# First batch's loads, first-stage PSUM banks, and the order and width of block sums in a linear-attention and mixture kernel

## Chip, cores, metric

One core of one Trainium2 chip. The metric is device time of one execution in microseconds; lower is better.

## The reference

A linear attention without softmax, with a normalisation by row, feeds four dense experts whose outputs are mixed by given probabilities. All data are fp32.

```python
kv  = einsum('bhsd,bhse->bhde', k, v)            # 8 batches, 8 heads, 576 rows, 64 columns
o   = einsum('bhsd,bhde->bhse', q, kv)
x   = o / sqrt(mean(o*o, -1) + 1e-6) * g_norm    # then heads side by side: x is 4608 x 512
p   = probs / probs.sum(-1)
out = sum over e of p[:, e] * (relu(x @ w1[e]) @ w2[e])   # w1: 512 x 1024, w2: 1024 x 512, 4 experts
```

## The kernel before

Each matrix product is done by two nested levels of a seven-product scheme (Strassen's form): blocks of w1, w2 and x are added and subtracted ahead ("block sums"), and products are added into the output blocks behind. x is handled in nine chunks of 512 rows. Expert 0 works through the nine chunks while the attention of the next batch runs in between; experts 1 to 3 read the chunks' x blocks back from DRAM. A pair of expert and chunk is a "step", 36 in all.

The kernel does not write instructions in order. It hands operations with a key (a place) and a cost to a planner, which simulates the engines and emits each engine's order. The parts that matter here:

```python
def either(n):        # a block sum may go to VectorE or to GpSimd, whichever is free in the plan
    return {"DVE": 0.17 + 0.00108 * n, "POOL": 0.1 + 0.0025 * n}
...
BANKS = {"ub": 4, "db": 2, "ab": 2}              # PSUM banks: up products, down products, attention
...
def weights_1(e, key, step):                     # w1 of expert e: four loads, then block sums
    ...
    form(key + 4 * step, 5, 21, 4, ALU.add)      # 1024-wide sums, both inputs in SBUF
    form(key + 5 * step, 6, 5, 1, ALU.subtract)
    form(key + 6 * step, 7, 1, 21, ALU.subtract)
    form(key + 7 * step, 3, 2, 6, ALU.subtract)
    for j, m in enumerate(OUTER):                # then four 256-wide sums for each of seven blocks
        k2 = key + (8 + j) * step
        ...combine(k2, either(HN), ...)
...
def total(a, t, src, add_, ...):                 # adds a product out of PSUM: VectorE only
    nc.vector.tensor_tensor(out=block(whole, a, t), in0=src.ap[:, 0:HN], in1=add_.ap[:], op=ALU.add)
...
attention(0, -2.0, 1.3, 0.1)
weights_1(0, -0.9, 0.02)
x_views = {0: x_forms(0, -0.2, 0.02)}
...
        if e + 1 < E and c == NCH - 1:           # next expert's weights, during the last chunk
            weights_1(e + 1, s + 0.0, 0.12)
            weights_2(e + 1, s + 1.0, 0.12)
```

Lines are named by number in the profiles (in some runs an edit shifts them by one or two). Before and after: block sums L276 and L279; up products L697 and L713; PSUM-fed sums L718 and L737; down products L831 and L850; merges into the output L784/L788 and L803/L807; attention's scaling L432 and L440, its powers L425 and L433.

## Time and profile before

| | before |
|---|---|
| median | 1820.93 us (6 runs, 1818.36 to 1821.4) |
| TensorE busy | 98% of 1818.3 us |
| work of TensorE at its steady pitch | 1757 us |
| lost by TensorE up to 130 us / 500 us / end | 44 / 52 / 57 us |
| each change of expert | 1.5 us lost |

"Lost" is a count of mine that the prediction sets up: the time on the clock, less the matmul records started by then, each at its steady pitch. Waits and a slow clock both show in it, which busy time does not do.

### The profile page before, as it was taken

How to read it: one execution, taken by the hardware profiler on the slowest of the kernel's cores; microseconds unless marked ns; L12 is line 12 of the kernel's file. 1: busy time of each engine (PE TensorE's matmuls, PEld its weight loads, DVE VectorE, ACT ScalarE, POOL GpSimd, SP SyncE). 2: the span in 40 equal slices, each digit the busy share in tenths (PEclk: the TensorE clock that was granted, in tenths of full speed). 3: DMA queues.
4: the chain of work that ended last, by engine and by line, in shares of the span. 5: the costliest groups of instructions: out<-in, count | busy, mean ns of one | idle time of the engine just before them, and what ended most of it. 6: DMA issues, size and time to landing. Idle time of an engine off the chain costs nothing.

```text
span 1818.3 us, 32290 instructions
## 1 busy us (share of the span) xinstructions
PE 1784.6 (98%) x12496; PEld 1660.7 (91%) x12496; DVE 1126.2 (62%) x1841; ACT 608.4 (33%) x1345; POOL 475.1 (26%) x426
## 2 busy tenths in 40 slices
PE   5899999999999999999999999999999999999999
PEld 4889999999999999999999999999999999999997
DVE  6866665666676555555666555555566655556554
ACT  2544344443333333333333333333333333333331
POOL 4565554646364000000145000000036100000001
PEclk7999999999999999999999999999999999999999
DMA  9764444424433333334434333333434333343321
GB/s 231 179 167 141 128 139 126 135 95 139 132 109 119 117 114 115 114 113 134 136 130 152 118 118 118 118 118 121 147 127 163 117 115 117 118 118 116 115 74 35
DMA packets 192089, 228.96 MB, mean 126 GB/s; under 512 B 54464, under 2 KB 123328, under 8 KB 191936
## 3 DMA queue, kind: packets, MB, share of 16 engines
q1 hardware_dynamic: 191936, 226.89, 40.9%
q8 instruction: 99, 1.62, 0.4%
q14 instruction: 54, 0.44, 0.1%
HBM read 160.18 MB, written 66.65 MB: 125 GB/s over the span
## 4 chain that ended last, share of the span: by engine, by line
PE 94%; DVE 2%; SPq 2%; DMA 1%; issue 1%; POOL 0%; ACT 0%; DVEq 0%; ACTq 0%
PE ub L697 42%; PE db L831 29%; PE ab L831 18%; SPq L282 1%; PE ab L504 1%; PE ab L486 1%; DVE big L276 1%; PE ab L514 1%; PE ab L471 1%; DVE small L276 0%; DMA big<-in_moe_w_dram 0%; DMA small<-in_q_dram 0%; PE ab L553 0%; DVE big L718 0%; POOL big L276 0%
## 5 line engine op out<-in xcount | busy, mean ns | idle before, releaser
L831 PE MATMUL db<-big,big 128*128 128x256 f32 x2520 | 596.3, 380 | 1.7 <-DVE big L276 1.3
L697 PEld LDWEIGHTS ub<-small,big 128*128 128x128 f32 x3816 | 498.4, 192 | 23.4 <-issue 1.4
L697 PE MATMUL ub<-small,big 128*128 128x128 f32 x3816 | 513.5, 276 | 0.4 <-DVE big L718 0.4
L276 DVE TENSOR_TENSOR big<-big,big 128x1024 f32<-128x1024 f32 x343 | 474.8, 1384 | 55.1 <-ACT big L680 33.2
L831 PEld LDWEIGHTS db<-big,big 128*128 128x128 f32 x2520 | 455.2, 190 | 51.7 <-DVE big L276 1.5
L276 POOL TENSOR_TENSOR big<-big,big 128x1024 f32<-128x1024 f32 x85 | 209.0, 2462 | 1116.7 <-DVE big L276 976.1
L710 ACT ACTIVATE snap<-ub 128x256 f32<-128x256 f32 x756 | 285.5, 383 | 556.7 <-PE ub L697 500.8
L718 DVE TENSOR_TENSOR big<-ub,snap 128x256 f32<-128x256 f32 x756 | 307.0, 421 | 216.7 <-PE ub L697 163.1
L697 PE MATMUL ub<-small,w1y 128*128 128x128 f32 x2916 | 384.9, 276 | 2.2 <-DVE big L718 2.1
L697 PEld LDWEIGHTS ub<-small,w1y 128*128 128x128 f32 x2916 | 360.5, 192 | 7.9 <-DVE big L718 2.9
L831 PE MATMUL ab<-big,big 128*128 128x256 f32 x1512 | 357.4, 380 | 1.7 <-DVE small L788 1.7
L831 PEld LDWEIGHTS ab<-big,big 128*128 128x128 f32 x1512 | 273.2, 190 | 32.0 <-DVE small L788 2.1
L710 ACT ACTIVATE big<-ub 128x256 f32<-128x256 f32 x252 | 96.7, 384 | 414.6 <-PE ub L697 410.1
L788 DVE SCALAR_TENSOR_TENSOR small<-db,p_all,small 128x256 f32<-128x256 f32 x243 | 116.9, 481 | 139.8 <-PE db L831 139.2
L788 DVE SCALAR_TENSOR_TENSOR small<-ab,p_all,small 128x256 f32<-128x256 f32 x189 | 91.1, 482 | 177.3 <-PE ab L831 177.3
L680 ACT ACTIVATE big<-big 128x1024 f32<-128x1024 f32 x144 | 152.0, 1055 | 107.8 <-DVE big L276 104.8
L784 DVE TENSOR_SCALAR small<-db,p_all 128x256 f32<-128x256 f32 x72 | 34.6, 481 | 54.1 <-PE db L831 54.1
L425 POOL TENSOR_TENSOR rt<-ss,mhalf 128x8 f32<-128x8 f32 (+1 forms) x40 | 65.7, 1643 | 3.3
L421 POOL TENSOR_SCALAR ss<-ss 128x8 f32<-128x8 f32 (+1 forms) x40 | 15.6, 391 | 101.0 <-DVE ss L416 99.6
L416 DVE TENSOR_REDUCE ss<-small 128x8 f32<-128x512 f32 (+1 forms) x40 | 27.1, 678 | 22.3 <-ACT small L411 22.3
L504 PE MATMUL ab<-kvbd,small 128*128 128x128 f32 x256 | 38.3, 298 | 1.6 <-ACT kvbd L494 1.6
L432 DVE TENSOR_TENSOR small<-ab,rt 128x512 f32<-128x512 f32 (+1 forms) x40 | 27.4, 686 | 17.3 <-POOL rt L425 17.1
(63 smaller groups left out, 664.0 us busy)
## 6 DMA issues: line engine op xcount, KB each, us to landing
small<-x SPq DMA_DIRECT2D x189, 256.0 KB, 3.5
small<-x SPq DMA_DIRECT2D x189, 192.0 KB, 2.9
o<-small SPq DMA_DIRECT2D x108, 256.0 KB, 2.0
small<-o SPq DMA_DIRECT2D x108, 256.0 KB, 2.8
big<-in_moe_w_dram SPq DMA_DIRECT2D x32, 512.0 KB, 5.0
x<-small SPq DMA_DIRECT2D x63, 256.0 KB, 3.1
small<-in_q_dram SPq DMA_DIRECT2D x72, 128.0 KB, 3.9
kv<-in_k_dram SPq DMA_DIRECT2D x32, 288.0 KB, 3.5
```

Source lines behind the costliest of these rows:

```text
L276: lambda eng: adder(eng).tensor_tensor(out=out_(), in0=a(), in1=b(), op=op),
L416: lambda eng: nc.vector.reduce_sum(out=ss.ap[0:n, :], in_=rows(sq), axis=AX.X),
L425: nc.gpsimd.tensor_tensor(out=rt.ap[0:n, :], in0=ss.ap[0:n, :], in1=mhalf[0:n, :], op=ALU.pow)
L432: lambda eng: nc.vector.tensor_tensor(out=rows(x), in0=rows(raw), in1=rt.ap[0:n, :].unsqueeze(2).to_broadcast([n, H, D]), op=ALU.mult,),
L504: nc.tensor.matmul(raw.ap[:, rs], lhsT=qT.ap[:, rs], rhs=kb.ap[:])
L680: lambda eng: nc.scalar.activation(out=b.ap[:], in_=b.ap[:], func=ACT.Relu),
L697: nc.tensor.matmul(ps.ap[:, u * P:(u + 1) * P], lhsT=w1f[e][m][mm][1]()[:, u * P:(u + 1) * P], rhs=views[m][mm][1](), start=(mm in (1, 2, ...
L710: lambda eng: nc.scalar.activation(out=where(), in_=ps.ap[:, 0:HN], func=ACT.Copy),
L718: lambda eng: nc.vector.tensor_tensor(out=block(whole, a, t), in0=src.ap[:, 0:HN], in1=add_.ap[:], op=ALU.add),
L784: nc.vector.tensor_scalar_mul(out=acc[i].ap[:, cols], in0=ps.ap[:, 0:HN], scalar1=prob)
L788: nc.vector.scalar_tensor_tensor(out=acc[i].ap[:, cols], in0=ps.ap[:, 0:HN], scalar=prob, in1=acc[i].ap[:, cols], op0=ALU.mult, op1=ALU.add,)
L831: nc.tensor.matmul(ps.ap[:, 0:HN], lhsT=four(h[m])[:, kt // 2, t, kt % 2, :], rhs=w2f[e][m].ap[:, kt * HN:(kt + 1) * HN], start=(m in (1, ...
```

## The change

Its intent: start TensorE earlier, by bringing the first batch's data ahead of the weights and using idle banks for its attention; then order the block sums by when their products need them, and merge some of them. The diff is cut to its main lines; lines that begin with `#` are comments of this text, and `...` marks what is left out within a line.

```diff
+    def add(..., after=()):                     # an op may be placed behind another in the plan
-  if len(free[k]) < n + (self.SPARE.get(k, 0) if op.key > front + 0.1 else 0):
+  if len(free[k]) < n + (self.SPARE.get(k, 0) if eng == "SP" and op.key > front + 0.1 else 0):
-    BANKS = {"ub": 4, "db": 2, "ab": 2}
+    BANKS = {"u1": 2, "u2": 2, "db": 2, "ab": 2}
 # weights_1: places by need, for every expert
-        form(key + 4 * step, 5, 21, 4, ALU.add)
-        form(key + 5 * step, 6, 5, 1, ALU.subtract)
-        form(key + 6 * step, 7, 1, 21, ALU.subtract)
-        form(key + 7 * step, 3, 2, 6, ALU.subtract)
+        form(need + 0.25, 5, 21, 4, ALU.add)
+        form(need + 0.26, 6, 5, 1, ALU.subtract)
+        form(need + 0.5, 7, 1, 21, ALU.subtract)
+        form(need + 0.5, 3, 2, 6, ALU.subtract)
-            k2 = key + (8 + j) * step
+            need + j / 7                         # (the 256-wide sums of block j)
 # first batch: its own buffers, loads first, other banks
-            kt, vt, qt = Buf("kv", f"k{n}"), Buf("kv", f"v{n}"), Buf("small", f"q{n}")
+            kind = "kv" if b or hp < 2 else "big"
+            kt, vt, qt = Buf(kind, f"k{n}"), Buf(kind, f"v{n}"), Buf("small", f"q{n}")
+            want = at(hp) - 0.25 if b else key - 1 + 0.1 * hp
+            ...Buf("ab" if b else "u1"...), Buf("ab" if b else "db"...), Buf("ab" if b else "u2"...)
 # x blocks: one 256-wide and two 128-wide sums for four 128-wide ones
-            for o, a, b in ((5, 12, 1), (6, 3, 5), (7, 3, 12), (4, 2, 6)):
+            combine(key + j / 7, either(2 * P), ...)
+            for o, a, b in ((6, 3, 5), (4, 2, 6)):
 # up products: at most about two blocks open
+                    after=last[-2:-1] if mm in (1, 2) else (),
 # calls
-    weights_1(0, -0.9, 0.02)
-    x_views = {0: x_forms(0, -0.2, 0.02)}
+    weights_1(0, -2.5, 0.02, -0.35)
+    x_views = {0: x_forms(0, -0.3)}
-                weights_1(e + 1, s + 0.0, 0.12)
+                weights_1(e + 1, s + 0.0, 0.12, s + 0.6)
```

More of the change, by code (lines that the diff above doesn't have):

```diff
@@ L49, in __init__, with add @@
         self.ops = []
-    def add(self, key, cost, fn, reads=(), writes=(), parts=(), kb=0):
+    def add(self, key, cost, fn, reads=(), writes=(), parts=(), kb=0, after=()):
         op = Op(key, cost, fn, reads, list(writes) + list(parts), kb)
+        for o in after:
+            op.deps[o] = True
         for b in reads:
@@ L67, in add @@
         self.ops.append(op)
+        return op
     def layout(self, slots):
@@ L278, in combine, with load @@
         )
-    def load(key, buf, dst, src, kb, reads=()):
+    def load(key, buf, dst, src, kb, reads=(), also=()):
         plan.add(
             key, SPC, lambda eng: nc.sync.dma_start(out=dst(), in_=src), reads=reads,
-            parts=[buf], kb=kb,
+            parts=[buf] + list(also), kb=kb,
         )
@@ L330, in w2_src, with weights_1 @@
         return rows.rearrange("(kt p) d -> p kt d", p=P)
-    def weights_1(e, key, step):
+    def weights_1(e, key, step, need):
         f = {n: Buf("big", f"w1_{e}_{n}") for n in (1, 2, 21, 4, 5, 6, 7, 3)}
+        corner = {}
         for i, (n, dh, uh) in enumerate(((1, 0, 0), (2, 1, 0), (21, 0, 1), (4, 1, 1))):
+            corner[n] = Buf(None, f"w1c_{e}_{n}")
             load(
@@ L338, in weights_1 @@
                 lambda n=n: f[n].ap[:].rearrange("p (k u) -> p k u", k=2),
-                w1_src(e, dh, uh), 512,
+                w1_src(e, dh, uh), 512, also=[corner[n]],
             )
         def form(k_, o, a, b, op):
+            corner[o] = Buf(None, f"w1c_{e}_{o}")
             combine(
                 k_, either(1024), lambda: f[o].ap[:], lambda: f[a].ap[:], lambda: f[b].ap[:], op,
-                [f[a], f[b]], [f[o]],
+                [f[a], f[b], corner[a], corner[b]], [f[o], corner[o]],
             )
-        form(key + 4 * step, 5, 21, 4, ALU.add)
-        form(key + 5 * step, 6, 5, 1, ALU.subtract)
-        form(key + 6 * step, 7, 1, 21, ALU.subtract)
-        form(key + 7 * step, 3, 2, 6, ALU.subtract)
+        form(need + 0.25, 5, 21, 4, ALU.add)
+        form(need + 0.26, 6, 5, 1, ALU.subtract)
+        form(need + 0.5, 7, 1, 21, ALU.subtract)
+        form(need + 0.5, 3, 2, 6, ALU.subtract)
         w1f[e] = {}
         for j, m in enumerate(OUTER):
-            x, y = f[m], Buf("w1y", f"w1y_{e}_{m}")
+            x, low, y = f[m], corner[m], Buf("w1y", f"w1y_{e}_{m}")
             parts = {}
-            for n, at, (uq, kt) in ((1, 0, (0, 0)), (2, 1, (0, 1)), (7, 2, (1, 0)), (4, 3, (1, 1))):
-                parts[n] = (x, lambda x=x, uq=uq, kt=kt: two(x.ap[:])[:, kt, uq * HN:(uq + 1) * HN])
+            for n, (uq, kt) in ((1, (0, 0)), (2, (0, 1)), (7, (1, 0)), (4, (1, 1))):
+                parts[n] = (
+                    [x, low] if n == 7 else [x],
+                    lambda x=x, uq=uq, kt=kt: two(x.ap[:])[:, kt, uq * HN:(uq + 1) * HN],
+                )
             for n, at in ((5, 0), (6, 1), (3, 2)):
-                parts[n] = (y, lambda y=y, at=at: y.ap[:, at * HN:(at + 1) * HN])
-            k2 = key + (8 + j) * step
+                parts[n] = ([y], lambda y=y, at=at: y.ap[:, at * HN:(at + 1) * HN])
             for o, a, b, op in (
@@ L365, in weights_1 @@
                 combine(
-                    k2, either(HN), parts[o][1], parts[a][1], parts[b][1], op,
-                    [parts[a][0], parts[b][0]], [parts[o][0]],
+                    need + j / 7, either(HN), parts[o][1], parts[a][1], parts[b][1], op,
+                    parts[a][0] + parts[b][0], [low] if o == 7 else [y],
                 )
@@ L445, in attention @@
             n = f"{b}_{hp}"
-            kt, vt, qt = Buf("kv", f"k{n}"), Buf("kv", f"v{n}"), Buf("small", f"q{n}")
+            kind = "kv" if b or hp < 2 else "big"
+            kt, vt, qt = Buf(kind, f"k{n}"), Buf(kind, f"v{n}"), Buf("small", f"q{n}")
+            want = at(hp) - 0.25 if b else key - 1 + 0.1 * hp
             def kv_rows(t):
-                return t.ap[0:KP, :].rearrange("p (h j d) -> p h j d", h=2, d=D)
+                return t.ap[0:KP, 0:2 * KR * D].rearrange("p (h j d) -> p h j d", h=2, d=D)
             for r in range(2):
                 load(
-                    at(hp) - 0.25, qt,
+                    want, qt,
                     lambda qt=qt, r=r: qt.ap[:].rearrange(
@@ L459, in attention @@
                 load(
-                    at(hp) - 0.25, t,
-                    lambda t=t: t.ap[0:KP, :].rearrange("p (h x) -> p h x", h=2),
+                    want, t,
+                    lambda t=t: t.ap[0:KP, 0:2 * KR * D].rearrange("p (h x) -> p h x", h=2),
                     src[b, hs].rearrange("h (p j) d -> p h (j d)", j=KR), 288,
@@ L479, in attention @@
             )
-            bank = Buf("ab", f"kv{n}")
+            bank = Buf("ab" if b else "u1", f"kv{n}")
             kvbd[hp] = Buf("kvbd", f"kvbd{n}")
@@ L497, in attention @@
             plan.add(at(hp), {"ACT": 0.5}, diagonal, reads=[bank], writes=[kvbd[hp]])
-            raw = Buf("ab", f"raw{n}")
+            raw = Buf("ab" if b else "db", f"raw{n}")
             def attend(eng, raw=raw, qT=qT, kb=kvbd[hp]):
@@ L508, in attention @@
             scaled(at(hp + 0.4), n, raw, P, x)
-            bank = Buf("ab", f"xT{n}")
+            bank = Buf("ab" if b else "u2", f"xT{n}")
             def turn_x(eng, bank=bank, x=x):
@@ L587, with x_forms @@
     kept = {}
-    def x_forms(c, key, step):
+    def x_forms(c, key):
         xh = x_halves(c)
@@ L601, in x_forms @@
             combine(
-                key + j * step, either(NT), blocks[o][1], blocks[a][1], blocks[b][1], ALU.subtract,
+                key + (0.25, 0.26, 0.65, 0.8)[j], either(NT), blocks[o][1], blocks[a][1], blocks[b][1], ALU.subtract,
                 [blocks[a][0], blocks[b][0]], [blocks[o][0]],
@@ L611, in x_forms @@
                 parts[n] = (src, lambda ap=ap, kt=kt, th=th: ap()[:, kt, th * P:(th + 1) * P])
-            for n, at in ((5, 0), (6, 1), (7, 2), (4, 3)):
+            for n, at in ((5, 0), (7, 1), (6, 2), (4, 3)):
                 parts[n] = (t, lambda t=t, at=at: t.ap[:, at * P:(at + 1) * P])
-            for o, a, b in ((5, 12, 1), (6, 3, 5), (7, 3, 12), (4, 2, 6)):
+            combine(
+                key + j / 7, either(2 * P), lambda t=t: two(t.ap[:, 0:2 * P]),
+                lambda ap=ap: ap()[:, :, P:2 * P], lambda ap=ap: two(ap()[:, 0, :]),
+                ALU.subtract, [src], [t],
+            )
+            for o, a, b in ((6, 3, 5), (4, 2, 6)):
                 combine(
-                    key + (4 + j) * step, either(P), parts[o][1], parts[a][1], parts[b][1],
-                    ALU.subtract, [parts[a][0], parts[b][0]], [parts[o][0]],
+                    key + j / 7, either(P), parts[o][1], parts[a][1], parts[b][1],
+                    ALU.subtract, [parts[a][0], parts[b][0]], [t],
                 )
@@ L626, in x_forms @@
             plan.add(
-                key + 0.5, {"SP": 0.16}, store_raw, reads=[src], parts=[kept[c, m]], kb=192,
+                key + 0.9, {"SP": 0.16}, store_raw, reads=[src], parts=[kept[c, m]], kb=192,
             )
             plan.add(
-                key + 0.5, SPC,
+                key + 0.9, SPC,
                 lambda eng, t=t, keep=keep: nc.sync.dma_start(out=keep[:, 3 * P:], in_=t.ap[:]),
@@ L651, in x_again @@
                 for n, b, at in (
-                    (1, r, 0), (2, r, 1), (3, r, 2), (5, t, 0), (6, t, 1), (7, t, 2), (4, t, 3)
+                    (1, r, 0), (2, r, 1), (3, r, 2), (5, t, 0), (7, t, 1), (6, t, 2), (4, t, 3)
                 )
@@ L658 @@
     hidden = {}
+    last = []
     def four(b):
@@ L686, in up @@
             whole = made[m] = Buf("big", f"m{n}")
-            bank = {1: Buf("ub", f"u1_{n}"), 2: Buf("ub", f"u2_{n}")}
+            bank = {1: Buf("u1", f"u1_{n}"), 2: Buf("u2", f"u2_{n}")}
             snap = {}
@@ L691, in up @@
                 if mm == 5:
-                    bank[2] = Buf("ub", f"u3_{n}")
+                    bank[2] = Buf("u2", f"u3_{n}")
                 ps = bank[1 if mm in (1, 6, 7, 4) else 2]
@@ L701, in product @@
                         )
-                plan.add(
-                    key, pe(2, P), product, reads=[w1f[e][m][mm][0], views[m][mm][0]], writes=[ps]
-                )
+                op = plan.add(
+                    key, pe(2, P), product, reads=w1f[e][m][mm][0] + [views[m][mm][0]], writes=[ps],
+                    after=last[-2:-1] if mm in (1, 2) else (),
+                )
+                if mm == 3:
+                    last.append(op)
                 def copy(to, where, ps=ps, key=key):
@@ L853 @@
     attention(0, -2.0, 1.3, 0.1)
-    weights_1(0, -0.9, 0.02)
-    x_views = {0: x_forms(0, -0.2, 0.02)}
+    weights_1(0, -2.5, 0.02, -0.35)
+    x_views = {0: x_forms(0, -0.3)}
     weights_2(0, 0.0, 0.02)
-    norm_probs(0.1)
+    norm_probs(0.3)
     for e in range(E):
@@ L867 @@
                 if e == 0 and c + 1 < NCH:
-                    x_views[s + 1] = x_forms(c + 1, s + 0.75, 0.03)
+                    x_views[s + 1] = x_forms(c + 1, s + 0.7)
                 else:
```

## The prediction

> **What bounds the kernel now.** I read the page first, then a table of busy times by stretch of the span, then the waits of the first 60 us, then the timeline of VectorE and GpSimd where VectorE is slow. The page has TensorE busy 98% and its clock low only at the beginning, so I cut the span into stretches:
>
> ```profile
> core 0: us, PE busy (x) PEld busy (x) DVE busy (x) ACT busy (x) POOL busy (x), PEclk, DMA share, GB/s
> 0.00:18.00 18.00, 9.96 (x76) 8.50 (x76) 2.99 (x12) 4.55 (x9) 2.55 (x8) 1.00 0.90 225
> 18.00:42.00 24.00, 12.43 (x91) 10.30 (x91) 21.04 (x35) 6.01 (x13) 16.43 (x15) 0.58 0.99 235
> 42.00:60.00 18.00, 14.88 (x123) 13.67 (x123) 17.26 (x29) 7.16 (x18) 14.50 (x18) 0.88 0.97 255
> 60.00:86.00 26.00, 23.84 (x244) 22.64 (x242) 20.60 (x32) 14.61 (x35) 9.12 (x7) 0.95 0.49 119
> 86.00:105.00 19.00, 18.43 (x158) 16.43 (x160) 13.75 (x26) 8.88 (x20) 18.08 (x19) 1.00 0.56 139
> 105.00:500.00 395.00, 394.51 (x3117) 363.94 (x3112) 254.43 (x428) 159.49 (x357) 207.29 (x236) 1.00 0.45 135
> 500.00:1814.00 1314.00, 1310.61 (x8703) 1225.21 (x8702) 795.90 (x1285) 407.73 (x895) 207.13 (x126) 1.00 0.37 118
> 1814.00:1818.30 4.30, 0.00 (x0) 0.00 (x0) 0.28 (x1) 0.00 (x0) 0.00 (x0) 0.85 0.47 107
> ```
>
> From 105 us on TensorE is full. Busy time hides slow clocks, so I count its work at the steady pitch of the chain of waits: 16 up-projection records took 1.79 us (0.112 each), 8 down-projection records 1.73 (0.216), one batch's attention about 12.3 us in all. The program has 7056 and 4032 such records and 8 batches: 788 + 871 + 98 = 1757 us. TensorE ends at 1813.8, so 56.6 us are lost and 4.5 us are tail. Counting the records finished by a given time, the loss is 13 us at 18, 31 at 41.8 (where the first up product starts), 37 at 60, 42 at 86, 43 at 105, 44 at 130, 52 at 500, 57 at the end. **Three quarters of what can be won lies before 86 us**; the rest is spread thin over 1700 us.
>
> What TensorE waits for in the first 60 us:
>
> ```profile
> PE ab L514 <- DVE small L432: 8.8, 3, 4.3
> PE ab L471 <- DMA small<-in_q_dram: 5.8, 1, 5.8
> PE ub L697 <- DVE big L718: 3.1, 2, 2.7
> PE ab L486 <- DMA kv<-in_v_dram: 1.8, 2, 1.6
> ```
>
> It waits for VectorE: the scaling of attention (L432), then block sums (L718). In 18 to 60 us VectorE is busy 38.3 of 42 us. But part of that is waiting, as the timeline of VectorE shows, beside GpSimd's in the same microseconds:
>
> ```profile
> 75.27 0.68 DVE L276 TENSOR_TENSOR small<-big 128x512 f32<-128x512 f32 x1
> 75.87 2.45 DVE L276 TENSOR_TENSOR small<-big,small 128x128 f32<-128x128 f32 x1
> 78.25 0.28 DVE L276 TENSOR_TENSOR small<-small 128x128 f32<-128x128 f32 x1
> ...
> 79.52 2.44 DVE L276 TENSOR_TENSOR small<-big,small 128x128 f32<-128x128 f32 x1
> ```
>
> ```profile
> 75.50 2.67 POOL L276 TENSOR_TENSOR big<-big,big 128x1024 f32<-128x1024 f32 x1 [4.38 <-DVE big L718]
> 79.45 2.35 POOL L276 TENSOR_TENSOR big<-big,big 128x1024 f32<-128x1024 f32 x1 [1.28 <-ACT big L680]
> ```
>
> A 128-wide sum of 0.28 us takes 2.4 us, until GpSimd's 1024-wide sum is done. So block sums with both inputs in SBUF run on one of the two engines at a time.
>
> **What the Trainium skill says.** "SBUF — State Buffer", section "Who interferes with whom": a VectorE instruction with two SBUF inputs contends with a GpSimd instruction that reads SBUF, and the later one blocks for the whole instruction. The lines above agree; so does the PSUM-fed sum (L718), which one SBUF input leaves out of it: 756 of them, none slower than 0.43 us. "GPSIMD Engine Reference", section "3.1 Elementwise — side-by-side cycle accounting", puts a two-input sum on GpSimd at 1.96 times VectorE's time; here the 1024-wide means are 2462 and 1384 ns, 1.8 times with VectorE's blocked ones in. "TensorE: Matmul & The Clock Gate", section "Part 1: The HAM clock gate", has TensorE at half clock until it has been busy some 3.4 us, and again after idling; here the clock is 0.58 in 18 to 42 us, where it idles, and four transposes take 1.1 us instead of 0.44.
>
> **The change, part by part.**
>
> *Loads.* k and v of the first batch's last two head pairs get buffers of their own and go ahead of w1. Before, they waited for the first two pairs' buffers and landed at 20.8 to 24.3 us, after w1 (15.4 to 19.8). Landings in that stretch follow each other by 1.0 to 1.3 us (288 KB) and 1.3 to 1.6 us (512 KB). Chained in the new order: v of the third pair lands at about 15.3, of the fourth at 18.7, w1 at 20 to 24.4. No bytes are removed; w1 comes 4.6 us later.
>
> *Banks.* The first batch uses six more PSUM banks, so its transposes need not wait for the previous scaling. I chain the new order of TensorE with the old durations: third pair's k·v 17.3 to 18.9, its attention to 21, fourth pair's k·v 21 to 22, its attention to 23.5. From the end of an attention product to x scaled took 12.82 to 16.93 = 4.1 us, so the last x is at 27.6. Before, the last two scalings stood behind a row of w1 sums on VectorE (at 33.9 and 39.2). With 0.7 us for the last transposes **the first up product starts at about 28.5 instead of 41.8 us: 13.3 us earlier.**
>
> *Sums by need.* But the w1 sums that VectorE did in 18 to 38 us now come after 24.8 us, among the products. Take the end of the first up projection (its last PSUM-fed sum was at 86.4 us). From the order of both programs I count VectorE from where the w1 work begins to that point. Before (18.2 us on): 24 sums of 256, 21 of 128, 9 of 1024, 3 of 512, 21 PSUM-fed, 12 attention steps. At unblocked start-to-start times (0.335, 0.20, 1.14, 0.60, 0.34, 0.6 us) with 1 us for the probabilities that is 39.7 us. It took 57.6 busy and 8.9 idle; 18 us were blocking. GpSimd's sums before that point (6 of 1024, 4 of 256, 2 of 512, 15 of 128) hold the port, by an estimate of 2.2, 0.55, 1.1 and 0.27 us each, for 21.6 us. After (24.8 on): 24 of 256, 14 of 128, 9 of 1024, 3 of 512, 21, 7 attention steps: 35.2 us. But the planner, which counts no blocking, gives GpSimd more: 8 of 1024, 13 of 256, 2 of 512, 4 of 128, which hold it 28 us. Scaled, VectorE is blocked 18 × 28/21.6 = 23 us: 24.8 + 35.2 + 23 = 83 us. Taking turns row by row gives me the same 83. With 2 us idle it is 85 instead of 86.4. By then GpSimd has made two more 1024-wide sums than before, some 4 us of port time not needed later. So **of the 13 us, about 5 remain**; VectorE and the port take the rest.
>
> *Wider sums.* Four 128-wide sums per x block become one 256-wide and two 128-wide: 63 instructions fewer in 9 chunks. In the contended stage 28 narrow ones go in pairs at 0.465 us, some 6.5 us per chunk; seven 256-wide and fourteen narrow ones are perhaps 1 us less. In chunks 1 to 8 this lies beside a full TensorE (394.5 of 395 us) and is worth nothing but slack: 0 to 1 us in all.
>
> *The rest.* Splitting the four up banks into two pairs, and the new ordering edge, leave late in the kernel the same distances between uses of a bank (in the programs' order, 83 against 86 up products within 0.9 to 1.35 us of the last use, none nearer). TensorE has the same 1757 us of work. The tail is untouched. Sum: 1821 − 5 − 1 = 1815.
>
> **The rivals.** (a) *The early start is kept whole.* If blocking is lighter than I scaled (GpSimd ends early, or its sums fall beside PSUM-fed ones), VectorE needs 24.8 + 35.2 + some 12 = 72 us and 12 to 14 us are won: 1808. For it: VectorE idled 8.9 us in 18 to 87 us, and half of that waiting for TensorE. Against it: 18 of a possible 22 us of GpSimd's holding did block before. (b) *Nothing is won*: w1 lands later, VectorE begins it 6.6 us later, GpSimd holds the port longer; the end of the first projection is at 87 to 90 us and TensorE merely waits inside it instead of ahead of it: 1820 to 1824. For it: the counts above. Against it: VectorE's 4.5 us less unblocked work. (c) *Half clock lasts longer*: waits between early products keep TensorE cold. Its 35 us in 28 to 85 us leave room even so: a us or two. (d) *New waits later* from the buffers that may now be taken without spare ones, or the paired banks; every us there counts fully, but the distances speak against it.
>
> **Range and chances.** Mine gives 1815, (a) 1808 or slightly better, (b) 1820 to 1824: 1806 to 1823. Faster by 2% needs under 1785.5, 36 us off. Even losing only what is lost by the first product (28.5 − 11 = 17.5), with the old 13.5 from 105 us on and the tail, gives 1757 + 17.5 + 13.5 + 4.5 = 1792. Slower by 2% would need 36 us of new waits. So 0.01, 0.98, 0.01.
>
> **What will show it.** First up product at 27 to 30 us; k, v of the last pairs landed by 19 us; the waits for L432 gone, those of up products for VectorE or GpSimd sums grown; VectorE's 1024- and 128-wide sums stretched in 28 to 80 us; the loss by my count 17 to 19 at the first product, back at 36 to 41 at the end of the first projection, and 8 more by 500 us as before. Wrong if that loss stays under 33 (rival a), or if it grows by more than 14 after 105 us (rival d).

## The result, and the profile after

**1837.13 us (6 runs, 1835.29 to 1840.48) against 1820.93: ratio 1.0092, 95% interval 1.0079 to 1.0105.** Slower by 0.9%, outside the range.

The stretches of the span again, the changed kernel. First column after the stretch's length: TensorE's busy time; then its weight loads, VectorE, ScalarE, GpSimd, the granted clock, DMA:

```profile
18.00:42.00 24.00, 14.85 (x121) 12.83 (x119) 19.56 (x28) 9.83 (x20) 19.93 (x17) 0.93 0.97 250
42.00:60.00 18.00, 12.49 (x76) 11.16 (x76) 17.11 (x23) 4.90 (x13) 11.81 (x9) 0.81 0.87 220
60.00:86.00 26.00, 19.38 (x196) 17.74 (x196) 23.15 (x38) 12.52 (x29) 18.07 (x14) 0.93 0.55 152
105.00:500.00 395.00, 395.00 (x3133) 364.40 (x3133) 253.28 (x411) 160.72 (x360) 214.88 (x210) 1.00 0.45 136
500.00:570.00 70.00, 65.32 (x424) 60.74 (x424) 45.25 (x66) 19.22 (x43) 37.03 (x26) 0.98 0.31 99
```

And one stretch of the kernel before that the prediction never cut out:

```profile
500.00:570.00 70.00, 68.70 (x458) 64.18 (x458) 44.10 (x70) 22.26 (x48) 40.43 (x32) 1.00 0.33 108
```

TensorE does more between 18 and 42 us than it did (14.85 against 12.43 us), then less between 42 and 86 (31.87 against 38.72). From 105 to 500 us it is full, as before. Then, between 500 and 570 us, where expert 0 gives way to expert 1, it idles 4.7 us instead of 1.3. In the loss count:

| lost, us | up to 40 | 60 | 90 | 130 | 500 | 500 to 600 | 900 to 1000 | 1300 to 1450 | end |
|---|---|---|---|---|---|---|---|---|---|
| before | 30.0 | 37.2 | 41.8 | 44.1 | 51.9 | +1.5 | +1.6 | +1.6 | 56.6 |
| after | 22.3 | 34.0 | 43.9 | 45.8 | 52.6 | +7.4 | +5.2 | +7.3 | 73.1 |

So there are two findings. **The early start came (7.7 us ahead at 40 us) and was given back by 90 us. And each of the three changes of expert costs 4 to 6 us more than before**, which makes 15 of the 16 us.

What TensorE waited for in the first 60 us of the changed kernel (total us, times, longest):

```profile
PE ab L481 <- DMA small<-in_q_dram: 6.4, 1, 6.4
PE u L713 <- DVE big L279: 6.1, 2, 3.9
PE u L524 <- DVE small L440: 4.5, 3, 2.9
PE u L713 <- DVE big L737: 3.1, 2, 2.4
```

The waits for attention's scaling halved (8.8 to 4.5); waits of up products for block sums took their place. The first up product is at 28.5 us.

The first change of expert, in the changed kernel: the timeline of VectorE (start, us, line, tiles, count),

```profile
521.57 0.42 DVE L737 TENSOR_TENSOR big<-u,snap 128x256 f32<-128x256 f32 x1
521.91 1.95 DVE L279 TENSOR_TENSOR w1y<-big 128x256 f32<-128x256 f32 x1
523.89 2.47 DVE L279 TENSOR_TENSOR big<-big 128x256 f32<-128x256 f32 x1
526.28 0.94 DVE L279 TENSOR_TENSOR w1y<-w1y,big 128x256 f32<-128x256 f32 x1
527.25 0.83 DVE L279 TENSOR_TENSOR w1y<-big,w1y 128x256 f32<-128x256 f32 x1
528.01 0.74 DVE L737 TENSOR_TENSOR big<-u,snap 128x256 f32<-128x256 f32 x2
```

GpSimd in the same microseconds,

```profile
521.23 4.85 POOL L279 TENSOR_TENSOR big<-big,big 128x1024 f32<-128x1024 f32 x2 [4.28 <-issue]
526.03 0.91 POOL L279 TENSOR_TENSOR w1y<-big 128x256 f32<-128x256 f32 x1
```

and TensorE:

```profile
528.47 0.71 PE L713 MATMUL u<-x_rem,big 128*128 128x128 f32 x4 [2.98 <-DVE big L737]
```

Four w1 sums of expert 1, 0.42 us each when nothing is in the way, take 6.2 us in all, because two 1024-wide sums of GpSimd stand before the first two. The PSUM-fed sum that would free TensorE's bank is behind them on VectorE, and TensorE waits 2.98 us. Its clock then falls as well; of the two stretches from 525 us on (same columns), the second has 0.51:

```profile
525.00:529.00 4.00, 1.02 (x9) 0.83 (x8) 3.97 (x6) 0.39 (x1) 3.59 (x4) 1.00 0.26 68
529.00:532.50 3.50, 3.50 (x15) 3.14 (x14) 2.35 (x4) 0.38 (x1) 0.72 (x1) 0.51 0.00 0
```

By estimate, 3.5 us at half clock cost another 1.7. The waits behind 105 us in the changed kernel are all of this kind: up products for PSUM-fed sums 9.5 us, down products for merges 5.1 us, in three repeats of the same pattern.

### The profile page after: what moved, and what is told of

Its sections match the earlier page's. It is cut to its first block, busy times and chain, and to the rows that moved or that the text cites. A ratio compares the mean times of both kernels' runs of the same rounds, so it can differ in the third digit from the quotient of the medians.

```text
span 1834.8 us, 32171 instructions
## 1 busy us (share of the span) xinstructions
PE 1785.6 (97%) x12496; PEld 1659.8 (90%) x12496; DVE 1147.1 (63%) x1824; ACT 608.1 (33%) x1345; POOL 475.2 (26%) x380
## 4 chain that ended last, share of the span: by engine, by line
PE 92%; DVE 5%; POOL 1%; issue 1%; SPq 0%; DMA 0%; DVEq 0%; POOLq 0%
PE u L713 41%; PE db L850 29%; PE ab L850 18%; DVE big L279 2%; DVE w1y L279 1%; PE ab L514 1%; PE ab L496 1%; DVE small L279 1%; PE ab L524 1%; POOL rt L433 1%; PE ab L481 1%; DVE big L737 0%; DMA big<-in_v_dram 0%; PE ab L563 0%; SPq L285 0%
## 5 line engine op out<-in xcount | busy, mean ns | idle before, releaser
L713 PEld LDWEIGHTS u<-small,big 128*128 128x128 f32 x3816 | 498.8, 192 | 35.0 <-DVE big L737 6.6
L713 PE MATMUL u<-small,big 128*128 128x128 f32 x3816 | 515.9, 276 | 12.2 <-DVE big L279 6.1
L279 DVE TENSOR_TENSOR big<-big,big 128x1024 f32<-128x1024 f32 x341 | 469.3, 1378 | 57.8 <-ACT big L696 38.4
L279 POOL TENSOR_TENSOR big<-big,big 128x1024 f32<-128x1024 f32 x87 | 212.1, 2444 | 1126.3 <-DVE big L279 992.5
L729 ACT ACTIVATE snap<-u 128x256 f32<-128x256 f32 x756 | 285.5, 383 | 523.7 <-PE u L713 445.0
L737 DVE TENSOR_TENSOR big<-u,snap 128x256 f32<-128x256 f32 x756 | 309.2, 421 | 219.6 <-PE u L713 158.4
L713 PE MATMUL u<-small,w1y 128*128 128x128 f32 x2916 | 389.1, 276 | 3.0 <-DVE big L737 2.9
L713 PEld LDWEIGHTS u<-small,w1y 128*128 128x128 f32 x2916 | 364.0, 193 | 10.5 <-DVE big L737 4.3
L729 ACT ACTIVATE big<-u 128x256 f32<-128x256 f32 x252 | 96.7, 384 | 455.1 <-PE u L713 452.1
L424 DVE TENSOR_REDUCE ss<-small 128x8 f32<-128x512 f32 (+1 forms) x40 | 27.1, 677 | 19.2 <-ACT small L419 18.7
L279 POOL TENSOR_TENSOR small<-big,small 128x128 f32<-128x128 f32 (+1 forms) x37 | 27.1, 733 | 45.2 <-DVE small L279 28.6
L279 POOL TENSOR_TENSOR small<-small 128x256 f32<-128x256 f32 x32 | 29.8, 931 | 31.4 <-PE u L713 19.0
```

The costliest lines, as they stand in the source:

```text
L279: lambda eng: adder(eng).tensor_tensor(out=out_(), in0=a(), in1=b(), op=op),
L424: lambda eng: nc.vector.reduce_sum(out=ss.ap[0:n, :], in_=rows(sq), axis=AX.X),
L713: nc.tensor.matmul(ps.ap[:, u * P:(u + 1) * P], lhsT=w1f[e][m][mm][1]()[:, u * P:(u + 1) * P], rhs=views[m][mm][1](), start=(mm in (1, 2, ...
L729: lambda eng: nc.scalar.activation(out=where(), in_=ps.ap[:, 0:HN], func=ACT.Copy),
L737: lambda eng: nc.vector.tensor_tensor(out=block(whole, a, t), in0=src.ap[:, 0:HN], in1=add_.ap[:], op=ALU.add),
```

## The experiments

All runs are of three rounds and with the right result, unless said. Each variant is planned anew by the kernel's planner, so an edit moves more than its own operations; I count an effect only where it is far over the few us by which plans differ anyhow. "Steps" are the loss at the three changes of expert (500 to 600, 900 to 1000, 1300 to 1450 us).

**Theory W** after the result: the new places of the w1 sums of experts 1 to 3 make the steps. Rivals: the paired banks with the ordering edge (B), or spare buffers now kept back for loads alone (S).

### 1. Old places of the w1 sums for experts 1 to 3

```diff
-        form(need + 0.25, ...)   # and the three others, and the 256-wide sums
+        form(key + 4 * step if e else need + 0.25, ...)
```

> The changed kernel, but experts 1 to 3 get the w1 sums at the old places of the plan (the first expert keeps the new ones). Theory W (the new places of the w1 sums cost 5 to 7 us at each of three expert changes): loss at 600 us falls from 60 to 53 to 55, at 1800 us from 72.6 to 57 to 60, time 1820 to 1824. Rival B (paired banks and the ordering edge): 1835 to 1839. Rival S (spare buffers now kept for loads only): 1835 to 1839.

Measured: 1823.45 us, ratio to before 1.0018. Steps 3.9, 0.7 and 1.8 us instead of 7.4, 5.2 and 7.3. As W expects; 14 of the 16 us are gone. Of the first step 2.4 us more than before stay here; in run 12, which also undoes the paired banks and the edge, they are gone too.

### 2. Only those places, in the kernel before

```diff
-        form(key + 4 * step, 5, 21, 4, ALU.add)        # and the three others
+        need = key + 0.6                                # key is s + 0.0, so this is the change's s + 0.6
+        fk = [need + d for d in (0.25, 0.26, 0.5, 0.5)] if e else [key + (4 + i) * step for i in range(4)]
+        form(fk[0], 5, 21, 4, ALU.add)                  # and the three others
-            k2 = key + (8 + j) * step
+            k2 = need + j / 7 if e else key + (8 + j) * step
```

> The kernel before, with only the places of the w1 sums of experts 1 to 3 moved as in the change. Theory W: the three steps of 5 to 7 us appear here too, 1833 to 1839, the first 500 us unchanged. Rivals B and S: 1819 to 1823, no steps.

Measured: 1835.14 us, ratio 1.0078. Steps 7.8, 6.1 and 6.3; up to 500 us the loss is that of before (52.2 against 51.9). So the new places alone make the steps: W is shown both ways. A place does more than set the time, since the planner also picks the engine by it: of the 84 256-wide w1 sums of experts 1 to 3, VectorE has 15 in the kernel before, 2 in run 1, and 27 in run 2 and in the changed kernel. So a move is of both at once; runs 9 and 10 below have the same engine and the same places.

### 3. One pool of four up banks, no ordering edge

```diff
-    BANKS = {"u1": 2, "u2": 2, "db": 2, "ab": 2}
+    BANKS = {"ub": 4, "db": 2, "ab": 2}
-                    after=last[-2:-1] if mm in (1, 2) else (),
+                    after=(),
```

> The changed kernel with one pool of four up banks again and without the ordering edge between up products; spare rule and places of sums as changed. Theory W: three steps remain, 1834 to 1840. Rival B: 1820 to 1825.

Measured: 1832.74 us, ratio 1.0063. Steps 7.1, 8.1 and 6.7: rival B falls as the cause of the steps. But the loss at 130 us is 42.6 instead of 45.8, so pairs and edge together cost the first stage about 3 us (run 12 against run 1 has the same direction, some 4 us), which the prediction had at nothing.

### 4. Spare buffers kept from every engine again

```diff
-  (self.SPARE.get(k, 0) if eng == "SP" and op.key > front + 0.1 else 0)
+  (self.SPARE.get(k, 0) if op.key > front + 0.1 else 0)
```

> The changed kernel with spare buffers kept back from every engine again, not from loads alone. Theory W: three steps remain, 1834 to 1840. Rival S: 1820 to 1825.

Measured: 1832.78 us, ratio 1.0068. Steps 7.0, 4.7 and 4.7. The main effect of S is not there; a part of the later steps may be.

**Theory G**: the steps, and the loss of the first stage too, come from VectorE's sums standing blocked behind GpSimd's. Rival L: too many sums too late for VectorE, whoever shares them.

### 5. The changed kernel, all block sums on VectorE

```diff
 def either(n):
-    return {"DVE": 0.17 + 0.00108 * n, "POOL": 0.1 + 0.0025 * n}
+    return {"DVE": 0.17 + 0.00108 * n}
```

> The changed kernel with every two-input block sum on VectorE alone; GpSimd keeps only the powers of attention. Theory G (at the expert changes VectorE's sums stand blocked behind GpSimd's 1024-wide ones, and the PSUM-fed sums behind them keep TensorE waiting): the three steps shrink to at most 3 us each, and the first stage gains too (loss at 130 us 36 to 43 instead of 46): 1808 to 1822. Rival L (the new places simply put too many sums too late for VectorE, whoever shares them): steps of 5 us or more stay or grow, 1835 to 1860.

Measured: 1803.79 us, ratio 0.9909, but a **wrong result** (relative error 0.041). The fault is one that both kernels carry: nothing orders the load of an output accumulator before the first merge into it, other than their places. In this plan the merge of step 9 is emitted before the load, which then overwrites it (found from the order in which the planner emits the two; the planner can be run without the chip). Run 10 mends that, with the same time. Steps 0.0, −0.2 and 0.0; loss at 130 us 33.6. Better than I had put it.

### 6. The kernel before, all block sums on VectorE

Same edit.

> The kernel before with every two-input block sum on VectorE alone. Theory G: the first stage is no worse without GpSimd (loss at 130 us 38 to 44 against 44), its three steps of 1.4 us at most the same: 1813 to 1821. Rival L: VectorE is too full alone, 1823 to 1850.

Measured: 1807.39 us, ratio 0.9927. Loss at 130 us 36.0 instead of 44.1, and no steps. Here I had the direction and half the size: taking GpSimd's help away from the old kernel is worth 13 us. The mean of VectorE's 1024-wide sums shows one reason. Groups of the changed kernel, then of run 8 (busy us, mean ns | idle before):

```profile
L279 DVE TENSOR_TENSOR big<-big,big 128x1024 f32<-128x1024 f32 x341 | 469.3, 1378 | 57.8 <-ACT big L696 38.4
```

```profile
L279 DVE TENSOR_TENSOR big<-big,big 128x1024 f32<-128x1024 f32 x428 | 520.7, 1219 | 25.9 <-ACT big L697 11.2
```

GpSimd had 87 of these 428 sums at 2444 ns each; VectorE does them for 51 us more busy time, and none of its 428 is over 1227 ns.

### 7. The first batch's part alone, in the kernel before

```diff
+            kind = "kv" if b or hp < 2 else "big"
-            bank = Buf("ab", f"kv{n}")
+            bank = Buf("ab" if b else "ub", f"kv{n}")       # and raw over "db", xT over "ub"
```

> The kernel before with only the first batch's part of the change: k and v of its last two head pairs in buffers of their own and its attention over the other banks; all sums at their old places and widths. If the early start survives: first up product at 28 to 33 us, loss at 130 us under 38, 1808 to 1814. If VectorE takes it back, as in the changed kernel: loss at 130 us 42 to 46, 1819 to 1823.

Measured: 1824.72 us, ratio 1.0024. First up product at 35.0 us instead of 41.8, loss at 130 us 50.4 instead of 44.1. The early start alone does not survive; it even costs, more than I expected in any case.

### 8. Changed kernel, old places for experts 1 to 3, all block sums on VectorE

Edits of runs 1 and 5.

> The changed kernel with the old places of the w1 sums for experts 1 to 3 and all block sums on VectorE alone. Theory G: start as in the run of the changed kernel without GpSimd, steps at most 2 us each: 1802 to 1815, below both kernels. Rival L: 1823 to 1850.

Measured: 1803.53 us, ratio 0.9906, right result. The stretches (columns as above):

```profile
42.00:60.00 18.00, 14.34 (x139) 13.50 (x140) 15.15 (x29) 6.94 (x19) 6.30 (x6) 0.77 1.04 270
60.00:86.00 26.00, 25.78 (x254) 23.78 (x254) 23.64 (x54) 13.86 (x35) 6.25 (x7) 1.00 0.68 174
500.00:570.00 70.00, 70.00 (x466) 65.46 (x465) 57.41 (x107) 20.00 (x46) 0.00 (x0) 1.00 0.40 127
```

TensorE is full from 60 us on, 254 records in 60 to 86 us against 196 in the changed kernel, with GpSimd's sums gone; VectorE is busy 23.64 us against 23.15, but with 54 instructions instead of 38. At the change of expert TensorE is busy 70.00 of 70 us. With the old places 1803.5 and with the new ones (run 10) 1803.9: **without GpSimd the places cost nothing.** So they hurt only where GpSimd shares the sums.

### 9. Only the w1 sums of experts 1 to 3 off GpSimd

```diff
-                k_, either(1024), ...    need + j / 7, either(HN), ...
+                k_, dve(1024) if e else either(1024), ...    need + j / 7, dve(HN) if e else either(HN), ...
```

> The changed kernel with only the w1 sums of experts 1 to 3 kept off GpSimd, at their new places. If what blocks VectorE at the expert changes is GpSimd's share of these very sums: steps of 3 us or less, 1823 to 1829. If it is GpSimd's other 1024-wide sums (w2 and the hidden units), behind which VectorE's w1 sums stand: steps of 5 us or more stay, 1834 to 1842.

Measured: 1839.78 us, ratio 1.0109. Steps 8.5, 7.3 and 8.2. So it is not GpSimd's share of these very sums that blocks. Here all 84 of the 256-wide w1 sums are VectorE's, as in run 10, and at the same places. VectorE in the first change of expert, and GpSimd with three 1024-wide sums in the same microseconds:

```profile
539.80 2.47 DVE L279 TENSOR_TENSOR w1y<-big 128x256 f32<-128x256 f32 x1
542.30 2.45 DVE L279 TENSOR_TENSOR big<-big 128x256 f32<-128x256 f32 x1
545.07 2.17 DVE L279 TENSOR_TENSOR w1y<-w1y,big 128x256 f32<-128x256 f32 x1
```

```profile
539.63 7.33 POOL L279 TENSOR_TENSOR big<-big,big 128x1024 f32<-128x1024 f32 x3 [4.75 <-DVE big L737]
```

### 10. Run 5 with the merge ordered after its load

```diff
-            plan.add(key - 0.4, {"DVE": 0.5}, fn, reads=[ps, probs], parts=[acc[i]])
+            plan.add(key - 0.4, {"DVE": 0.5}, fn, reads=[ps, probs], parts=[acc[i]],
+                     after=[got[i]] if e else ())            # got[i]: the load of acc[i]
```

> The changed kernel without GpSimd's sums, as the run that gave a wrong result, and with the missing order of the first merge after the load of its accumulator. Right result; if that load was the fault and no part of the gain, the time is the same, 1802 to 1807. If the gain came from the missing wait: 1812 or more.

Measured: 1803.86 us, ratio 0.9908, right result. The fault was no part of the gain. Its steps are 0, as in run 5, and TensorE has no listed wait behind 105 us. Against run 9, which has the same w1 sums on VectorE at the same places, only GpSimd's sums are gone (and the merge is mended): so it is these, and neither the late places nor VectorE's larger share of the w1 sums as such, that make the steps.

### 11. Narrow x sums again

```diff
-            combine(key + j / 7, either(2 * P), ...)         # 256-wide pair
-            for o, a, b in ((6, 3, 5), (4, 2, 6)):
+            for o, a, b in ((5, 12, 1), (7, 3, 12), (6, 3, 5), (4, 2, 6)):
```

> The changed kernel with four 128-wide sums per x block again instead of one 256-wide and two 128-wide. By the prediction's step: worth 0 to 1 us, so 1836 to 1840, loss at 130 us 45 to 48. If the wider sums matter more while the port is contended: loss at 130 us 49 or more, over 1841.

Measured: 1846.9 us (1841.64 to 1847.84), ratio 1.0138. Loss at 130 us 51.6 instead of 45.8, steps 7.4, 7.0 and 8.4. My 0 to 1 us for the wider sums was far too small: in this plan they are worth some 6 us in the first stage. How much of that is the sums themselves and how much the plan they lead to, this run does not tell.

### 12. Old places and one pool, GpSimd kept

Edits of runs 1 and 3.

> The changed kernel with the old places of the w1 sums for experts 1 to 3 and one pool of four up banks without the ordering edge; GpSimd keeps its share. If the two effects add: 1837 less 14 less 4, 1816 to 1822. If the pool's gain of the first stage is a matter of one plan only: 1822 to 1827.

Measured: 1817.28 us, ratio 0.9984 (0.9967 to 1.0). Steps about 0.6, 1.0 and 0.9. The two effects add. The change's intent, with its two harmful parts undone, is worth some 3 us (by the interval, between 0 and 6).

### 13. The other sums off GpSimd, w1 sums shared

```diff
-                key, either(2 * NT), ...     # hidden units' sums
+                key, dve(2 * NT) if s >= 8 else either(2 * NT), ...
-                k_, either(1024), ...        # in weights_2
+                k_, dve(1024) if e else either(1024), ...
```

> The changed kernel with the other way round: from step 8 on the hidden units' sums and the w2 sums on VectorE, the w1 sums at their new places still shared with GpSimd. Theory G2 (VectorE's w1 sums stand behind GpSimd's 1024-wide hidden-unit and w2 sums): steps of 3 us or less, 1819 to 1828, the first stage as changed (loss at 130 us 44 to 47). Rival (any GpSimd sum beside the newly placed w1 sums does it, the w1 forms themselves too): steps of 4 us or more stay, 1831 to 1840.

Measured: 1818.26 us, ratio 0.9989. Steps 2.0, 0.7 and 0.8, loss at 130 us 44.7. This agrees with runs 9 and 10: the newly placed w1 sums stood behind GpSimd's 1024-wide sums of the hidden units and of w2. By itself it would not settle it, since the planner also gives VectorE fewer of the w1 sums here (15 of 84 instead of 27), and it does not tell the hidden units' sums from those of w2. VectorE at the same change of expert in this run:

```profile
520.56 0.94 DVE L737 TENSOR_TENSOR big<-u,snap 128x256 f32<-128x256 f32 x2
521.42 0.42 DVE L279 TENSOR_TENSOR w1y<-w1y,big 128x256 f32<-128x256 f32 x1
521.87 0.42 DVE L279 TENSOR_TENSOR w1y<-big,w1y 128x256 f32<-128x256 f32 x1
522.42 0.87 DVE L737 TENSOR_TENSOR big<-u,snap 128x256 f32<-128x256 f32 x2
```

w1 sums of 0.42 us again, and no PSUM-fed sum waits long behind them.

### 14. A try for a better version: no GpSimd sums, old places, one pool with the edge, merge after load

Edits of runs 8, 3 (the banks only) and 10.

> A try for a better version: no GpSimd sums, old places of the w1 sums of experts 1 to 3, one pool of four up banks, ordering edge kept, merge after load. If the paired banks cost the first stage 3 us here as they do with GpSimd: 1799 to 1802. If that cost came with blocking only: 1802 to 1806.

Measured: 1803.15 us (1802.84 to 1803.92), ratio 0.9907. Not told apart from run 8 (0.9906): the paired banks cost little or nothing once GpSimd does not block. It beats the two kernels by 17 and 34 us, and it also mends the missing order. (The same without the edge could not be planned: the planner found no operation that could start. This comes from the planner, not from a run.)

## Why the prediction was wrong

**Right, and how far.** The loads: w1 landed at 21.1 to 26.5 us (predicted 20 to 24.4), the last v at 19.9 (18.7). The first up product came at 28.5 us, as predicted to the tenth; that the tenth agrees is luck, the chain was not that exact. VectorE was busy 57.9 us from 24.5 us to the end of the first up projection (predicted 58). The mechanism, that blocking by GpSimd takes the early start back, was right: less the 35.2 us of unblocked work counted in the prediction, VectorE was blocked some 23 us, as I scaled it. (The scaling had a slip in it: 57.6 busy and 8.9 idle do not fill the stretch from 18.2 to 86.4 us, for which the trace has 59.1 and 9.1. With 19 us of blocking before instead of 18, it would have given 25.)

**The first stage, mis-sized.** The end of the first up projection is its 21st PSUM-fed sum:

```profile
86.94 0.42 DVE L737 TENSOR_TENSOR big<-u,snap 128x256 f32<-128x256 f32 x1 [0.80 <-PE u L713]
```

So it came at 87.4 us, not at 85, and behind the 86.4 of the kernel before: VectorE was idle 5.0 us on the way where I had 2. From there I counted on "some 4 us of port time not needed later", because GpSimd was two wide sums ahead. It did not come: the loss stood at 43.9 at 90 us against 41.8 before, where I had 36 to 41 at the end of the projection; TensorE waited another 3.9 us for the next batch's attention up to 82 us. Of the 5 us that should remain, −1.7 did. That is rival (b), whose 87 to 90 us came true. Within it the term "*Wider sums* ... 0 to 1 us in all" was wrong as well, in the other direction (run 11), and the paired banks with their edge cost some 3 us where I had none (run 3).

**The step that failed.** It is "*The rest*". There I wrote that the bank distances late in the kernel are the same, that TensorE has the same work, and that the tail is untouched, and went on to the sum. All three hold. What I left out is that the new places of the w1 sums are in a function called for every expert. I priced them only for the first. At each later change of expert they put short VectorE sums with two SBUF inputs between the PSUM-fed sums that TensorE needs, at the time when GpSimd runs its 1024-wide ones. Runs 1 and 2 show that this move alone makes the 14 to 15 us, and runs 9 and 10 that it does so through GpSimd's other sums: with the w1 sums all on VectorE at the new places, the steps are 7 to 9 us beside those sums and 0 without them. Run 13 agrees. Rival (d), "new waits later", is what happened; I tied it to buffers and banks, and looked there only. The mechanism that I had set out for 18 to 86 us was the right one for 520, 940 and 1370 us too.

**What I took as given.** GpSimd's help was a fixed condition in my working: I counted 28 us of port time as the price of the sums it does. VectorE does the same sums in less (a 1024-wide one in 1.22 us instead of 2.4), so the help was itself a cost: runs 5, 6 and 8, without it, lose 8 to 12 us less in the first 130 us.

**Left open.** A loss of 6 to 8 us between 130 and 500 us is in every run, with TensorE full; it may be a pitch that my count puts too low for attention's mixture of products. Whether the w1 sums suffer more from their later places or from VectorE's larger share of them, beside GpSimd's sums, no run tells: one with all of them on VectorE at the old places and GpSimd's other sums kept is missing.

## What to carry to other kernels

When a change alters a function, list every call of it and price each, and cut the trace at each of those places before predicting. Before moving sums between engines, look at whether the two engines can run them at the same time at all: here a plan that counted two engines as two was slower by 13 us (the kernel before) and 33 us (the changed one) than one that used VectorE alone for the block sums. A short operation is dangerous where an operation that TensorE waits for is next in the same queue (2.98 us of waiting behind sums of 0.42).

## What the Trainium skill lacked or had wrong

- "SBUF — State Buffer", "Who interferes with whom", has the blocking right (1.95 and 2.47 us for sums of 0.42), but gives no size for what it amounts to when two-input sums are shared out: giving all block sums, 428 of them 1024-wide, to VectorE took 0.7% (run 6) and 1.8% (run 10 against the changed kernel: 1803.86 and 1837.13 us) off the time.
- The same page, "SBUF: two separate sides", has the shared pair held for the whole instruction by whichever starts first. GpSimd's power instructions (8 elements in each partition, two SBUF inputs, 1.64 us) did not do so: in run 8, 29 VectorE block sums began inside one, and none took over 0.01 us more than its usual time.
- "TensorE: Matmul & The Clock Gate", "Part 1: The HAM clock gate", gives an idle window of about 3.4 us, free-running, before half clock, but not how much of a window must be idle. In the changed kernel a wait of 2.98 us was followed by 3.4 us at half clock at two of the three changes of expert, the first and the last, and not at the second. The clock's records change at 529.06, 532.47, 1372.15 and 1375.56 us, a grid of 3.41 us. In the grid's stretch just before the half clock TensorE waited 2.8 and 2.0 us; at the second change the grid cuts the wait into 1.4 and 1.6.
